# First seed requests on ScalarE's queue, and all seed stages three slots sooner, in a kernel of an S4D convolution beside softmax attention

## The chip, the cores and the metric

The kernel runs on one core of a Trainium2 chip. The metric is device time of one execution in microseconds, the lower the better. PE is TensorE, PEld its weight loads, DVE is VectorE, ACT is ScalarE, POOL is GpSimd and SP is SyncE, which here only requests DMA transfers. ACT can request transfers too, on a queue of its own.

## The reference

Two independent layers on sequences of 2048 with 448 channels, all in float32, concatenated at the end:

```python
dt = jnp.exp(log_dt)                                   # 448 step sizes
A = -jnp.exp(log_A_real) + 1j * A_imag                 # 448 x 256 poles
C = (C_real + 1j * C_imag) * dt[:, None]
P = jnp.exp((A * dt[:, None])[:, :, None] * pos[None, None, :])
K = 2.0 * jnp.einsum("dn,dnl->dl", C, P).real          # 448 x 2048 convolution kernel
y = irfft(rfft(u_t, L2) * rfft(K, L2), L2)[:, :, :L]   # causal convolution of u
a = y + u * D_skip
...
qkv = (x @ wqkv) ...                                   # 16 heads of 28
p = softmax(einsum("bhqd,bhkd->bhqk", q, k) * scale)
b = einsum("bhqk,bhkd->bhqd", p, v) ... @ wo
return jnp.concatenate([a, b], axis=-1)
```

## The kernel before

The kernel has three stages. In the opening stage it projects x to queries, keys and values and at the same time computes the seeds of the convolution kernel. In a short second stage (the maximum pass) it finds the row maxima of the first block of scores. In the main loop, 1054 of 1283 us, it does the attention and, in slots between the attention's steps, builds K from the seeds, transforms u and multiplies the spectra.

**The projections.** x comes in four parts of 512 rows (`load_x`, c = 0 to 3). Each part is transposed on PE (`transposes`), split into a high and a low half (`xh` by ACT, `xl` by DVE), and multiplied with the weights, which are split the same way: `khat` holds the halves of the query and key weights for now, in the space that later holds the first keys, and `vh`, `vl` those of the value weights. The weights arrive in two staging tiles of the pool name `tri`, which the seeds use later. A part gives 12 jobs, 48 in all: `qk_proj` for keys (s = 1) and queries (s = 0) of four groups, and four `v_proj`. What a job left in PSUM (`pm`) is evacuated behind the next job's matmuls: high half by ACT, low half by DVE (`hl`, in the last part `xn` for queries), then written to DRAM. For the keys of the first two parts a difference is made as well (`kb`, `dhl`), with POOL making the low half of it. Once the last matmul has read a group's weights, keys are loaded back into `khat`, four rows' requests for each of four indexes.

**The seeds.** The 448 channels are eight octets of 56. `seeds(o)` lists the stages of octet o: load four parameter arrays (`nat`), exponential and scaling by the step sizes (`exp_a`, `times_dt`), transposes to PSUM (`turn`, tile `pn`), phases and sizes (`phases`, `sizes`, both into a `tri` tile), `reduce`, `sines`, then `g_base` (POOL; `gz`), `places`/`e_base` (POOL, in `qhat` tiles), `e3` and `g_first` (DVE; `px`, `sg`), `e5` (POOL; `x_e`), `g_copies` (ACT; `sg`), and two writes to DRAM (`put_g`, `put_e`). Every octet needs two table loads of ACT, one for the exponential and one for the sine. The step sizes are made once for all octets: `exact_exp` computes their exponential by some twenty small DVE instructions on 8 x 56 numbers, `turn_dt` transposes it, and five copies fill `dt_all`.

**What sets the order.** The opening stage is written in slots (lines 534 to 583). Slot t first issues projection jobs until 48 (t + 1)/37 of them are out (`PW` = 37), then the seed stages that fall into it: stage i of octet o stands in slot 4 o + i (`SP` = 4), its load two slots ahead of the octet's first. So there are 41 slots; the last four hold only seed stages of the last octet. After slot 36 the last keys, values and the next query block are loaded. In this stage the order written is a priority: a planner with a cost model of its own sorts the instructions of each engine, in the end each engine runs its list in order. Only ACT's table functions are tied in program order (`in_order`). In the main loop the order written is kept on every engine.

SP requests nearly all transfers, in order: the identity, the first part of x, the weights, a column of ones, the step sizes (`log_dt`, tile `sg`), octet 0's four parameter arrays, then `pw2` (powers of two, which `phases` needs) and constants.

Of the kernel before, what the change touches and what calls it, by code (L numbers as in the profile page):

```python
# [18 lines left out]
D = 448  # L19

H = 16
DH = 28
G = 4
HG = H // G
# [3 lines left out]
CK = 112  # L28
NCK = D // CK
# [20 lines left out]
JF = DF // 4  # L50
NB = D // 8
NBF = NB // 2
NO = 8
BO = NB // NO
PO = BO * 8
LV = 11
# [34 lines left out]
def body(ctx, tc, a, out):  # L91
    nc = Engines(tc)
    nc.kept = KEPT["p"]
    x, wqkv, wo, u_a = a["B_x"][0], a["B_wqkv"], a["B_wo"], a["A_u"][0]
# [23 lines left out]
    sel = const.tile([128, HG], F32, name="sel")  # L118
    kones = const.tile([128, 1], F32, name="kones")
# [106 lines left out]
    with ExitStack() as st:  # L226
        sst, xst, wst = ExitStack(), ExitStack(), ExitStack()
        t_p = pool(sst, "t_p")
# [16 lines left out]
        load_x(0)  # L245
        w_g = k0_t[:CK].rearrange("p g (i s k h e) -> p i s k g h e", i=2, s=2, k=NCK, h=HG)
        vh = y_p.tile([CK, NCK, D], F32R, name="vh")
        vl = y_p.tile([CK, NCK, D], F32R, name="vl")
        nc.gpsimd.memset(k0_t[:CK].rearrange("p g (n e) -> p (g n) e", e=32)[:, :, DH:].bitcast(F32), 0.0)
        vst = [x_p.tile([128, H, 32], F32, name=f"vst{i}") for i in range(2)]  # L250
        for t in vst:
            nc.gpsimd.memset(t[:, :, DH:DH + 1], 1.0)
            nc.gpsimd.memset(t[:, :, DH + 1:], 0.0)
        wns = []
        for i in range(2):
            wn = t_p.tile([128, 3, LV, BO * 16], F32, name="tri", bufs=2).rearrange("p t k h -> p (t k h)")
            wn = wn[:CK, :2 * 3 * D].rearrange("p (k s d) -> p k s d", k=2, s=3)
            wns += [wn[:, 0], wn[:, 1]]
        for k in range(NCK):
            nc.sync.dma_start(wns[k], wqkv[k * CK:(k + 1) * CK, :].rearrange("p (s d) -> p s d", s=3))  # L260
# [5 lines left out]
        def load_nat(o):  # L266
            nats[o] = s_p.tile([PO, 4, 256], F32, name="nat", bufs=2)
            for i, n in enumerate(("A_log_A_real", "A_A_imag", "A_C_real", "A_C_imag")):
                nc.sync.dma_start(nats[o][:, i, :], bass.AP(tensor=a[n].tensor, offset=a[n].offset + first(o) * 256,
                                                            ap=[[256, JF // 4], [JF * 256, 4], [1, 256]]))  # L270
# [4 lines left out]
        ldt = next(small)  # L275
        t = a["A_log_dt"]
        for f in range(2):
            nc.sync.dma_start(ldt[4 * f:4 * f + 4, :].rearrange("o (j i) -> o j i", j=4), bass.AP(
                tensor=t.tensor, offset=t.offset + f * DF, ap=[[JF // 4, 4], [JF, 4], [1, JF // 4]]))
        load_nat(0)  # L280
        pw2 = s_p.tile([128, LV], F32, name="pw2")
        nc.sync.dma_start(pw2, a["pw2"])
        half_pi = s_p.tile([128, 1], F32, name="half_pi")
        nc.gpsimd.memset(half_pi, TWO_PI / 4)
        nc.sync.dma_start(sel, a["sel"])
        nc.sync.dma_start(w1, a["w1"])
        for k in range(NCK):
            for s in (1, 0):
                src = wns[k][:, s, :].rearrange("p (g h e) -> p g h e", g=G, e=DH)
                hi, lo = (w_g[:, i, s, k, :, :, :DH] for i in range(2))  # L290
                nc.scalar.activation(hi, src, AF.Copy)
                nc.vector.tensor_tensor(lo, src, hi.bitcast(F32), ALU.subtract)
            nc.scalar.activation(vh[:, k, :], wns[k][:, 2, :], AF.Copy)
            nc.gpsimd.tensor_tensor(vl[:, k, :], wns[k][:, 2, :], vh[:, k, :].bitcast(F32), ALU.subtract)

        def exact_exp(y, x_, shape):

# [22 lines left out]
        def turn_dt():  # L320
            dt_ps = ps_t.tile([128, CQ], F32, name="pt")[:PO, :NO]
            nc.tensor.transpose(dt_ps, dt_o, ident[:NO, :NO])
            for i, f in enumerate((1.0, 0.15915494309189535, 2.0, -2.0, -1.0)):
                nc.vector.tensor_scalar(dt_all[:, i, :], dt_ps, f, None, op0=ALU.mult)

        NH = BO * 16
        mul = lambda e, o_, x_, y_: e.tensor_tensor(o_, x_, y_, ALU.mult)
# [215 lines left out]

        ahead = collections.defaultdict(list)
# [624 lines left out]
```

## Time and profile before

| | us |
|---|---|
| median of 3 runs | 1283.33 |
| lowest, highest | 1280.13, 1284.64 |
| the profiled execution | 1284.67 |
| its span | 1282.8 |

| engine | busy us | share of the span |
|---|---|---|
| PE | 1223.7 | 95% |
| ACT | 967.8 | 75% |
| DVE | 925.5 | 72% |
| POOL | 843.4 | 66% |

The profile is of one execution. Its span runs from the first to the last instruction recorded; the execution's own time is 1.9 us longer. The views that are quoted are of four kinds. A row of the order of time has the start and the length in us, the engine, the operation, the tiles written and read (buffer numbers left out), the shapes, how many instructions were merged, and in brackets how long the engine idled ahead of it and what ended that. All rows name line 75, a helper through which every instruction goes, so tiles tell them apart. A row of a tile has a group's least, median and greatest length in ns, and the start of its first and last instruction. A row of stretches has the busy time of each engine in a part of the span. A row of the DMA requests has their count and the KB of each. SPq and ACTq stand for requests of transfers, whose length is that of the request and not of the transfer.

### The profile page before, as it was taken

What the parts mean: (1) busy time and instruction counts of PE and PEld (TensorE: products, weight loads), DVE (VectorE), ACT (ScalarE), POOL (GpSimd) and SP (SyncE); (2) the same over time, 40 slices, a digit from 0 to 9 for tenths busy, and PEclk for the clock granted to TensorE, in tenths of its full rate; (3) what the DMA queues carried; (4) which work ended last, traced back from release to release, by engine and by line L of the source; (5) the groups of instructions that cost most, each with busy time, mean ns of one, the idle gap of its engine ahead of it and who ended that gap; (6) DMA issues with size and microseconds to landing.
All of it is one profiled execution on the core that took longest, in us unless ns stands there. A gap on an engine that the chain in (4) does not pass through costs nothing.

```text
span 1282.8 us, 33335 instructions
## 1 busy us (share of the span) xinstructions
PE 1223.7 (95%) x12641; PEld 700.9 (55%) x12641; DVE 925.5 (72%) x2106; ACT 967.8 (75%) x2162; POOL 843.4 (66%) x728
## 2 busy tenths in 40 slices
PE   7988867999999999999999999999999999999987
PEld 5867754455555555555555555555555555544433
DVE  5788877787877787878778888888887645645111
ACT  4978856688888888888888888888887666656452
POOL 2466651798778888877689999989995222324321
PEclk9988888899999999999999999999999999999999
DMA  6767887446664544465533223432324533657665
GB/s 210 263 242 241 265 301 290 127 93 182 172 154 106 156 133 146 128 214 195 169 102 91 61 76 106 149 88 71 83 59 154 175 135 132 205 171 227 194 171 165
DMA packets 200089, 205.36 MB, mean 160 GB/s; under 512 B 95992, under 2 KB 158520, under 8 KB 197880
## 3 DMA queue, kind: packets, MB, share of 16 engines
q1 hardware_dynamic: 199720, 202.87, 51.4%
q8 instruction: 100, 1.64, 0.5%
q10 hardware_dynamic: 208, 0.36, 0.1%
q14 instruction: 61, 0.50, 0.1%
HBM read 120.73 MB, written 82.18 MB: 158 GB/s over the span
## 4 chain that ended last, share of the span: by engine, by line
PE 77%; DVE 7%; ACT 5%; POOL 5%; issue 3%; DMA 2%; SPq 0%; ACTq 0%; POOLq 0%; DVEq 0%
PE pm L75 44%; PE pss L75 16%; PE po L75 16%; POOL e L75 1%; ACT tri L75 1%; DVE mx L75 1%; ACT rl L75 1%; PE pt L75 1%; POOL qhat L75 1%; DVE sg L75 1%; DVE hl L75 1%; DVE tri L75 1%; POOL x_e L75 1%; DVE px L75 1%; POOL p L75 1%
## 5 line engine op out<-in xcount | busy, mean ns | idle before, releaser
L75 ACT ACTIVATE p<-pss 128x512 f32<-128x512 f32 x1024 | 561.4, 611 | 112.8 <-PE pss L75 108.5
L75 PE MATMUL pss<-qhat,khat 128*128 128x512 f32 x1024 | 402.7, 399 | 1.5 <-ACT p L75 1.4
L75 DVE TENSOR_REDUCE mx<-pm 128x1 f32<-128x512 f32 x480 | 308.6, 684 | 109.6 <-PE pm L75 107.5
L75 PE MATMUL pm<-khat,qhat 128*128 128x512 f32 x749 | 326.4, 439 | 5.3 <-ACT rl L75 3.0
L75 POOL TENSOR_TENSOR e<-e,sdb 128x256 f32<-128x256 f32 x168 | 201.9, 1202 | 108.1 <-ACT e L75 62.4
L75 PE MATMUL po<-p,v 128*32 128x512 f32 x2048 | 269.1, 594 | 0.0
L75 POOL TENSOR_TENSOR e<-e,eu 128x256 f32<-128x256 f32 x168 | 248.0, 1476 | 13.2
L75 PEld LDWEIGHTS pm<-khat,qhat 128*128 128x128 f32 x749 | 141.4, 189 | 201.3 <-ACT p L75 52.0
L75 DVE CUSTOM_DVE_ANT_0 rl<-pm,rl 128x512 f32<-128x512 f32 x259 | 178.4, 689 | 71.6 <-ACT rl L75 68.4
L75 PEld LDWEIGHTS pss<-qhat,khat 128*128 128x128 f32 x1024 | 190.4, 188 | 46.1 <-issue 10.8
L75 POOL TENSOR_TENSOR eu<-e,sdb 128x256 f32<-128x256 f32 x168 | 202.0, 1202 | 0.0
L75 POOL TENSOR_TENSOR p<-pr,pr 64x448 f32<-64x448 f32 x64 | 73.1, 1142 | 160.4 <-PE pm L75 135.2
L75 ACT ACTIVATE rl<-pm 128x512 f32<-128x512 f32 x259 | 157.1, 607 | 12.7 <-PE pm L75 7.9
L75 DVE TENSOR_TENSOR g<-g,zg 128x128 f32<-128x128 f32 x392 | 162.2, 414 | 3.4
L75 PE MATMUL pm<-kdif,qhat 128*128 128x512 f32 x249 | 101.1, 406 | 8.5 <-DVE xn L75 6.6
L75 PE MATMUL pm<-xh,khat 112*128 112x512 f32 x256 | 87.0, 422 | 9.2 <-DVE kb L75 4.4
L75 DVE TENSOR_TENSOR zg<-g,zg 128x128 f32<-128x128 f32 x224 | 87.9, 393 | 5.1
L75 PEld LDWEIGHTS pm<-e,g 128*32 128x32 f32 x3584 | 57.2, 109 | 43.8 <-issue 16.1
L75 DVE TENSOR_TENSOR pr<-pm,ub 128x448 f32<-128x448 f32 x64 | 37.0, 620 | 56.2 <-PE pm L75 41.8
L75 PE MATMUL pm<-e,g 128*32 128x64 f32 x3584 | 73.0, 222 | 1.9 <-POOL e L75 1.9
L75 ACT ACTIVATE y<-pm 128x448 f32<-128x448 f32 x48 | 26.5, 553 | 58.2 <-PE pm L75 34.1
L75 ACT ACTIVATE ub<-pm 128x224 f32<-128x224 f32 (+1 forms) x96 | 38.8, 450 | 39.9 <-PE pm L75 37.6
(134 smaller groups left out, 1465.5 us busy)
## 6 DMA issues: line engine op xcount, KB each, us to landing
sdb<-sd SPq DMA_DIRECT2D x55, 336.0 KB
qhat<-q SPq DMA_DIRECT2D x64, 256.0 KB
khat<-k SPq DMA_DIRECT2D x64, 256.0 KB
sd<-sg SPq DMA_DIRECT2D x8, 1456.0 KB
k<-hl SPq DMA_DIRECT2D x16, 512.0 KB
mw<-in_mw SPq DMA_DIRECT2D x16, 512.0 KB
sd<-qhat SPq DMA_DIRECT2D x8, 896.0 KB
yu_d<-ub SPq DMA_DIRECT2D x64, 112.0 KB
```

Source lines behind the costliest of these rows:

```text
L75: i = f(*args, **kw)
```

## The change

Five things change.

The requests for the step sizes and for octet 0's four arrays go out on ACT's queue, ahead of the first part of x and the weights on SP's. The memset of `half_pi` moves with them. The exponential of the step sizes is written ahead of the weights and their splits. `pw2` is requested before the column of ones. All seed stages stand three slots sooner (`SH` = 3): stage i of octet o in slot 4 o + i - 3, its load in slot 4 o - 5, nothing sooner than slot 0, so that octet 0's first four stages share slot 0, behind `turn_dt`. There are 38 slots instead of 41, and the projection jobs keep their slots.

```diff
-S0, SP, SW, SD, PW, E3 = 0, 4, 0, 5, 37, 8
+SP, SH, PW, E3 = 4, 3, 37, 8
...
+        def load_nat(o, queue=nc.sync):
+            nats[o] = s_p.tile([PO, 4, 256], F32, name="nat", bufs=2)
+            for i, n in enumerate(("A_log_A_real", "A_A_imag", "A_C_real", "A_C_imag")):
+                queue.dma_start(nats[o][:, i, :], bass.AP(...))
...
+        for f in range(2):
+            nc.scalar.dma_start(ldt[4 * f:4 * f + 4, :].rearrange("o (j i) -> o j i", j=4), bass.AP(
+                tensor=t.tensor, offset=t.offset + f * DF, ap=[[JF // 4, 4], [JF, 4], [1, JF // 4]]))
+        load_nat(0, nc.scalar)
+        half_pi = s_p.tile([128, 1], F32, name="half_pi")
+        nc.gpsimd.memset(half_pi, TWO_PI / 4)
...
+        dt8 = next(small)
+        exact_exp(dt8, ldt, [NO, PO])
+        dt_o = next(small)
+        nc.vector.tensor_copy(dt_o.rearrange("o (i j) -> o j i", j=4), dt8.rearrange("o (j i) -> o j i", j=4))
...
         load_x(0)
...
         for k in range(NCK):
             nc.sync.dma_start(wns[k], wqkv[k * CK:(k + 1) * CK, :].rearrange("p (s d) -> p s d", s=3))
-        nc.sync.dma_start(kones, a["kones"])
...
         pw2 = s_p.tile([128, LV], F32, name="pw2")
         nc.sync.dma_start(pw2, a["pw2"])
+        nc.sync.dma_start(kones, a["kones"])
...
-        n_stage = SP * (NO - 1) + len(stages[0])
+        n_stage = SP * (NO - 1) + len(stages[0]) - SH
...
-                slots[max(SP * o + (i or -2), 0)] += st_
-        slots[1].insert(0, turn_dt)
+                slots[max(SP * o + (i - SH if i else -2 - SH), 0)] += st_
+        slots[0].insert(1, turn_dt)
```

The lines that were taken from their old places (the same requests on SP's queue, and the text of `exact_exp` and `turn_dt`, which is unchanged) are left out.

More of the change, by code (lines that the diff above doesn't have):

```diff
@@ L324, in turn_dt @@
                 nc.vector.tensor_scalar(dt_all[:, i, :], dt_ps, f, None, op0=ALU.mult)
+        load_x(0)
+        w_g = k0_t[:CK].rearrange("p g (i s k h e) -> p i s k g h e", i=2, s=2, k=NCK, h=HG)
+        vh = y_p.tile([CK, NCK, D], F32R, name="vh")
+        vl = y_p.tile([CK, NCK, D], F32R, name="vl")
+        nc.gpsimd.memset(k0_t[:CK].rearrange("p g (n e) -> p (g n) e", e=32)[:, :, DH:].bitcast(F32), 0.0)
+        vst = [x_p.tile([128, H, 32], F32, name=f"vst{i}") for i in range(2)]
+        for t in vst:
+            nc.gpsimd.memset(t[:, :, DH:DH + 1], 1.0)
+            nc.gpsimd.memset(t[:, :, DH + 1:], 0.0)
+        wns = []
+        for i in range(2):
+            wn = t_p.tile([128, 3, LV, BO * 16], F32, name="tri", bufs=2).rearrange("p t k h -> p (t k h)")
+            wn = wn[:CK, :2 * 3 * D].rearrange("p (k s d) -> p k s d", k=2, s=3)
+            wns += [wn[:, 0], wn[:, 1]]
+        for k in range(NCK):
+            nc.sync.dma_start(wns[k], wqkv[k * CK:(k + 1) * CK, :].rearrange("p (s d) -> p s d", s=3))
+        pw2 = s_p.tile([128, LV], F32, name="pw2")
+        nc.sync.dma_start(pw2, a["pw2"])
+        nc.sync.dma_start(kones, a["kones"])
+        nc.sync.dma_start(sel, a["sel"])
+        nc.sync.dma_start(w1, a["w1"])
+        for k in range(NCK):
+            for s in (1, 0):
+                src = wns[k][:, s, :].rearrange("p (g h e) -> p g h e", g=G, e=DH)
+                hi, lo = (w_g[:, i, s, k, :, :, :DH] for i in range(2))
+                nc.scalar.activation(hi, src, AF.Copy)
+                nc.vector.tensor_tensor(lo, src, hi.bitcast(F32), ALU.subtract)
+            nc.scalar.activation(vh[:, k, :], wns[k][:, 2, :], AF.Copy)
+            nc.gpsimd.tensor_tensor(vl[:, k, :], wns[k][:, 2, :], vh[:, k, :].bitcast(F32), ALU.subtract)
         NH = BO * 16
```

35 lines of the change are left out of this document (2 added, 33 removed).

## The prediction

> **What bounds the kernel now.** I read the page's head first, then the busy time by stretch, because the change touches only the opening stage.
>
> ```profile
> span 1282.8 us, 33335 instructions
> 0.00:181.00 181.00, 158.00 (x705) 126.97 (x705) 138.31 (x266) 140.47 (x337) 93.44 (x131) 0.94 0.74 248
> 181.00:196.00 15.00, 2.54 (x5) 1.34 (x5) 11.71 (x25) 4.08 (x15) 13.77 (x20) 0.57 1.02 359
> 196.00:228.00 32.00, 26.20 (x79) 15.09 (x79) 22.21 (x67) 19.99 (x37) 0.82 (x1) 0.87 0.68 248
> 228.00:1282.00 1054.00, 1036.94 (x11852) 557.45 (x11852) 753.28 (x1749) 803.24 (x1776) 735.39 (x578) 1.00 0.47 140
> ```
>
> The columns are the stretch, its length, the busy time of PE, PEld, DVE, ACT and POOL, the granted clock, the DMA share and GB/s. From 228 us on PE is busy 1036.94 of 1054 us. That is the main loop; the change leaves its instructions and their order alone, so it only starts sooner or later. Up to 181 us PE does the projections and is busy 158.00 of 181 us. Between them lies a hole: in 181 to 196 us PE works 2.54 of 15 us, while DVE works 11.71 and POOL 13.77. What they do there is read in the order of time, first ACT's own, then PE's, then the DMA requests.
>
> ```profile
> 183.36 0.57 ACT L75 ACTIVATE sg<-pn 128x112 f32<-128x112 f32 x2 [3.54 <-DVE px L75]
> 186.88 0.39 ACT L75 ACTIVATE gz<-gz 128x224 f32<-128x224 f32 x1 [1.92 <-POOL gz L75]
> 187.18 0.54 ACT L75 ACTIVATE sg<-px 128x112 f32<-128x112 f32 x2
> 187.52 0.63 ACT L75 ACTIVATE xn<-pm 128x512 fp32r<-128x512 f32 x1
> 192.93 0.58 ACT L75 ACTIVATE sg<-pn 128x112 f32<-128x112 f32 x2 [4.78 <-DVE px L75]
> 195.01 0.57 ACT L75 ACTIVATE sg<-px 128x112 f32<-128x112 f32 x2 [1.50 <-DVE sg L75]
> 195.37 0.63 ACT L75 ACTIVATE rl<-pt 128x512 f32<-128x512 f32 x1
> ...
> 179.81 0.40 PE L75 MATMUL pm<-xl,khat 112*128 112x512 f32 x1
> 181.90 0.47 PE L75 MATMUL pt<-kdif,qhat 128*128 128x512 f32 x1 [1.70 <-issue]
> 188.93 0.79 PE L75 MATMUL pm<-kdif,qhat 128*128 128x512 f32 x1 [6.56 <-DVE xn L75]
> 196.06 1.53 PE L75 MATMUL pt<-khat,qhat 128*128 128x512 f32 x2 [5.05 <-ACT rl L75]
> ...
> 179.11 3.02 SPq L75 DMA_DIRECT2D khat<-k  x4
> 189.43 6.82 SPq L75 DMA_DIRECT2D khat<-k  x8
> ```
>
> The `sg` and `gz` copies are seed stages: those at 183.36 and 187.18 belong to octet 6, those at 192.93 and 195.01 to octet 7, the last. ACT runs in order, so two things stand behind them. The last projection's evacuation, `xn<-pm`, starts only at 187.52, and its DVE half holds PE for 6.56 us. The first `rl` of the maximum pass starts at 195.37, right behind octet 7's last copy, and holds PE for 5.05 us. So in this stretch the tail of the seeds ends last, not the matrix work. PE has no seed work in the hole at all.
>
> **The change part by part.** The sum is made against the profiled execution: 1284.67 us, 1.9 more than its span and 1.3 above the median of 1283.33. I carry differences over to the median.
>
> *How far three slots are.* The same step of the octets gives the pace.
>
> ```profile
> L75 DVE TENSOR_TENSOR tri<-pn,pw x8: 1425/1440/1444, 34.5 to 165.1; 128x1232 f32<-128x1232 f32 x8
> ```
>
> Eight octets lie 130.6 us apart from first to last, 18.7 us each, 4.66 us per slot; three slots are 14.0 us. The last copy at 195.58 would come at 181.6, as the projections end, instead of 15 us behind.
>
> *Step 1, the first requests.* Six requests (two for the step sizes, four of `nat`) leave SP's queue, where they stood behind the weights, and go out on ACT's queue ahead of x's and the weights' data.
>
> ```profile
> 1.19 0.93 SPq L75 DMA_DIRECT2D xn<-in_B_x  x2
> 4.66 2.23 PE L75 MATMUL pt<-ident,xn 128*112 128x128 f32 x8 [4.66 <-DMA xn<-in_B_x]
> 4.63 1.60 SPq L75 DMA_DIRECT2D sg<-in_A_log_dt  x2
> 6.28 1.02 SPq L75 DMA_DIRECT2D nat<-in_A_log_A_real  x1
> 9.52 0.83 SPq L75 DMA_DIRECT2D nat<-in_A_A_imag  x1
> 9.53 1.04 ACT L75 ACTIVATE khat<-tri 112x448 fp32r<-112x448 f32 x2 [2.44 <-DMA tri<-in_B_wqkv]
> ...
> nat<-in_A_log_A_real SPq DMA_DIRECT2D x8, 56.0 KB
> ...
> 4.60:9.10 4.50, 2.18 (x8) 1.38 (x8) 0.69 (x1) 0.60 (x1) 0.00 (x0) 1.00 0.98 296
> 9.10:13.80 4.70, 3.55 (x10) 2.89 (x11) 3.06 (x6) 3.98 (x8) 1.66 (x2) 1.00 1.02 264
> ```
>
> The DMA engines are full (0.98 and 1.02) while PE waits for the weights, so four times 56 KB ahead of them cost 224 KB at 264 GB/s, 0.85 us. Against this, SP gets those requests out of its way (its second `nat` request went out only as the first weights landed, 9.52 against 9.53), which releases `pw2`, the constants and the next x; none was waited for. The bounds are 0, if the seeds' rows run beside x without holding a weight, and +2.4, if a weight request must also wait for the step sizes to land: x itself landed at 4.66 after a request at 1.19, 3.5 us, so up to 1.5 us more. I take +0.9, nearest to the full DMA share.
>
> The Trainium skill's page "DMA: Bandwidth & Descriptors", section "Issuing engines are not separate DMA queues", says that requests of the scalar and the sync engine end on the same 16 DMA engines and interleave. By that rule the +0.9 is right; if ACT's queue were a way of its own it would be 0 and the total 0.9 us lower. The trace agrees as far as it goes: the share is already at 1.02 with one queue in use. On ACT the six requests take about 1.60 + 1.02 + 0.83 + 2 x 0.8 = 5.1 us by SP's own rows, about 6 us from the start. ACT's first copy that waits for weights is at 9.53, after 2.44 us of idling: hidden, with some 3 us to spare.
>
> *Step 2, the exponential ahead of the weights.*
>
> ```profile
> L75 DVE TENSOR_SCALAR sg<-sg x10: 167/175/180, 21.1 to 27.1; 8x56 f32<-8x56 f32 x10
> L75 DVE TENSOR_TENSOR sg<-sg x6: 196/204/643, 23.5 to 27.3; 8x56 f32<-8x56 f32 x6
> L75 DVE SCALAR_TENSOR_TENSOR sg<-sg x3: 203/204/204, 21.7 to 27.5; 8x56 f32<-8x56 f32 x3
> L75 DVE TENSOR_TENSOR khat<-tri,khat x8: 615/621/1575, 10.1 to 19.6; 112x448 fp32r<-112x448 f32 x8
> 28.33 0.45 DVE L75 TENSOR_SCALAR dt_all<-pt 56x8 f32<-56x8 f32 x5 [0.35 <-PE pt L75]
> ```
>
> 10 x 0.175 + 6 x 0.204 + 3 x 0.204 plus two copies of about 0.2 is 4.0 us of DVE, moved from 21 to 28 us to about 5 to 9 us, where DVE works 0.69 of 4.50. Behind it on DVE stand the first `xl` and the weights' low halves, made from 10.1 us on. If the step sizes landed as late as 6.5 us, the low halves would slip by 0.4 us; taken as 0. The freed 4 us at 21 to 28 us are filled again by the first octet's phases: 0. The step sizes' transpose and five copies now come before the first scaling, as they did; 0.
>
> *Step 3, all stages three slots sooner.* The tail leaves the hole. With nothing of the seeds ahead of them, the last evacuations follow the last projection at their own 0.6 and 0.7 us, and the maximum pass starts about 2 to 3 us after PE's last projection at 180.2 instead of at 196.06. Five of its 80 matmuls (16 tiles of five) were already done in the hole, worth 5/80 of 32 us, 2.0 us. So the gain is 196.06 - 2.0 - 183 = 11; less 1 us for matmuls that find their key rows still loading, 10 us. Ends: -14, the full three slots, and 0. The loads aren't late: the key rows of indexes 0 and 1 are requested from 179.11 on, each index feeds a quarter of the pass (8 us), and the eight requests at 189.43 serve indexes 2 and 3, needed 16 and 24 us in. The DMA share of 1.02 in the hole says that they can't come much sooner, which is why I do not take -14.
>
> The "TensorE: Matmul & The Clock Gate" page of the Trainium skill (section "Part 1: The HAM clock gate") says the array halves its clock after about 3.4 us of idling and needs as long to come back. The trace agrees: 0.57 in the hole. By the rule a gap of 2 to 3 us would keep the clock, and the pass would not begin with 3.4 us at half speed, an estimate by that page of up to 1.7 us more; the sum doesn't use it.
>
> *Step 4, what the moved work costs where it goes.* About 11.7 us of DVE, 13.8 of POOL and 4 of ACT move in under the projections, which leave 181 - 138.31 = 42.7, 87.6 and 40.5 us free. But engines run in order, and one wait of this kind is there already:
>
> ```profile
> 71.65 2.15 POOL L75 TENSOR_TENSOR x_e<-qhat 128x336 f32<-128x336 f32 x1 [1.32 <-DVE qhat L75]
> L75 POOL TENSOR_TENSOR dhl<-kb,dhl x8: 723/736/1003, 24.7 to 88.0; 128x256 fp32r<-128x256 f32 x8
> L75 POOL TENSOR_TENSOR gz<-tri x8: 653/936/1000, 41.7 to 186.2; 128x224 f32<-128x224 f32 x8
> 76.82 0.72 POOL L75 TENSOR_TENSOR dhl<-kb,dhl 128x256 fp32r<-128x256 f32 x1
> 77.57 0.38 ACT L75 ACTIVATE kb<-pm 128x256 f32<-128x256 f32 x1 [4.73 <-POOL dhl L75]
> 78.47 1.22 PE L75 MATMUL pm<-xh,khat 112*128 112x512 f32 x2 [4.39 <-DVE kb L75]
> ```
>
> A projection's `dhl` stood on POOL behind octet 1's powers, and PE lost 4.39 us. There are eight such `dhl`, from 24.7 to 88.0, all in the first two passes over x. Shifted seeds can meet more of them or miss this one: bounds -4.4 and +13 (three more). I take +2, half of one, since the first three or four lay ahead of the seeds' POOL work, which began at 41.7 and now begins some 14 us sooner.
>
> Sum: +0.9 + 0 - 10 + 2 = -7.1 us. Profiled 1284.67 - 7.1 = 1277.6; median 1283.33 - 7.1 = **1276.2 us**.
>
> **The rivals.**
>
> *The tail stays where the planner puts it.*
>
> ```profile
> 176.56 0.41 DVE L75 TENSOR_TENSOR qhat<-qhat 128x112 f32<-128x112 f32 x1
> ```
>
> This is octet 6's `e3` (program slot 33), 11.5 us behind octet 7's `tri<-pn,pw` at 165.1 (slot 32), and so octet 6's copies of slot 34 ran as late as 187.7. If the new last octet lags the same, its copies, now in slots 34 and 35, end one slot later than octet 6's did: 187.7 + 4.7 = 192.4 against 195.58, a gain of 3.2, less 0.9: -2.3 us, 1281.0. For it speaks that the lag arose under the projections, with three slots to go. Against it: POOL and DVE were half idle there, so the lag is one of order, and the planner sorts anew.
>
> *POOL's seeds get in the way of `dhl` (slower).* Place: 25 to 60 us. With POOL's seeds from about 28 us instead of 41.7, the `dhl` of the first pass meet the powers of octet 0, as one of the second pass met octet 1's. Price 4.39 us of PE each, as quoted. Beyond two more stalls than before the gain is gone; with four it is -9.1 + 17.6 = +8.5, 1291.8; with three, 1287.4. For it: the wait exists. Against: POOL is busy 93.44 of 181 us, and only one of eight was caught so far.
>
> *The seeds' requests aren't what starts the seeds.* The first `phases` writes a `tri` buffer that holds weights until their splits end, near 20.3 us (the last at 19.6). `tri<-pn,pw` can then move from 34.5 to about 21, 13.5 instead of 14.0 us: -6.6, 1276.7, inside the forecast.
>
> **How the numbers follow.** Forecast (5 to 11 us faster) 0.54; more, with the `dhl` stall missed, 0.06; tail still late (1 to 5 us faster) 0.19; POOL in the way (slower) 0.21. A measurement tells about 0.3%, 3.9 us, from no change. Faster: 0.54 + 0.06 + 0.04 of the late tail = 0.64. Within: the rest of the late tail and a little of the POOL case, 0.17. Slower: 0.19. The forecast's own range is 1272 to 1279; over all cases 1270.5 to 1287, leaving out most of the large POOL case and the very large gain.
>
> **What would show it.** Step 1: the first `khat<-tri` at 9.5 moves to about 10.4. Step 2: the `sg<-sg` group starts near 5 us, not 21. Step 3: `tri<-pn,pw` runs from about 20 to 151, the last `sg<-px` copy lies near 182, the first `rl` near 184, and PE in the 15 us behind the projections is busy over 10 us. Step 4: the waits of PE for `kb`, `hl` and `xl` sum to within 3 us of before. I would be wrong if PE's busy share up to the end of the projections fell, pushing that end beyond 186 us, or if ACT still copied `sg` ahead of the first `rl`.

## The result and the profile after

The change made the kernel faster by less than half of what was forecast, going by the measured ratio. It is 0.9975, 95% interval 0.9967 to 0.9983, which is 3.2 us; the forecast was 1276.2 us, a ratio of 0.9944, 7.1 us. The medians of nine runs each, 1283.33 us before and 1278.39 us after (1277.67 to 1279.79), lie 4.9 us apart; but in the later rounds the kernel before had medians of 1281.0 to 1281.7 us, which fits the smaller figure. The profiled executions differ by more, 6.2 us of span: the one of the kernel before, 1284.67 us, is the slowest of all its executions measured, so part of what the profiles show below as gained is the luck of that execution. The time after lies inside the range, and the gain is below the 0.3% that the prediction took as the least a measurement can tell.

The busy time by stretch, the kernel after, same columns as before:

```profile
span 1276.6 us, 33328 instructions
0.00:181.00 181.00, 154.88 (x681) 122.00 (x682) 141.04 (x277) 140.87 (x343) 104.51 (x144) 0.93 0.75 245
181.00:196.00 15.00, 11.98 (x43) 8.37 (x41) 9.55 (x23) 7.98 (x17) 6.05 (x6) 0.89 1.01 354
196.00:228.00 32.00, 25.02 (x78) 13.63 (x76) 23.41 (x70) 17.43 (x32) 0.43 (x1) 0.87 0.92 326
228.00:1276.00 1048.00, 1032.06 (x11844) 555.32 (x11843) 749.03 (x1740) 801.28 (x1771) 735.19 (x578) 1.00 0.48 139
```

The hole is filled: PE is busy 11.98 of the 15 us from 181 on, where it was busy 2.54. But up to 181 us it is busy 154.88 us, 3.1 less than before. Part of what fills the hole is projection work that came late. The order of time shows it, ACT's rows first and then PE's:

```profile
185.15 0.58 ACT L75 ACTIVATE sg<-pn 128x112 f32<-128x112 f32 x2 [0.29 <-DVE px L75]
187.76 0.57 ACT L75 ACTIVATE sg<-px 128x112 f32<-128x112 f32 x2 [2.03 <-DVE sg L75]
188.13 0.63 ACT L75 ACTIVATE xn<-pm 128x512 fp32r<-128x512 f32 x1
188.66 0.59 ACT L75 ACTIVATE rl<-pt 128x512 f32<-128x512 f32 x1
...
186.53 0.40 PE L75 MATMUL pm<-xl,khat 112*128 112x512 f32 x1
189.54 0.80 PE L75 MATMUL pm<-kdif,qhat 128*128 128x512 f32 x1 [2.37 <-DVE xn L75]
```

The last projection ends at 186.9 us instead of 180.2, the last copy of the seeds at 188.3 instead of 195.6, and the first `rl` starts at 188.66 instead of 195.37. ACT still has octet 7's copies ahead of the first `rl`; now projections and seeds end almost together. The start, in order of time and by tile:

```profile
10.27 1.04 ACT L75 ACTIVATE khat<-tri 112x448 fp32r<-112x448 f32 x2 [1.30 <-DMA tri<-in_B_wqkv]
17.78 0.90 ACT L75 ACTIVATE nat<-nat,dt_all 56x256 f32<-56x256 f32 x2
20.12 0.90 ACT L75 ACTIVATE nat<-nat,dt_all 56x256 f32<-56x256 f32 x2
...
L75 DVE TENSOR_SCALAR sg<-sg x10: 172/178/438, 2.8 to 6.4; 8x56 f32<-8x56 f32 x10
L75 DVE TENSOR_TENSOR tri<-pn,pw x8: 1422/1437/1456, 25.7 to 157.9; 128x1232 f32<-128x1232 f32 x8
```

The exponential runs at 2.8 us instead of 21. The eight octets' phases start 8.8 us sooner at the first and 7.2 us sooner at the last, not 14.

**One account for all kernels.** In every kernel below, the maximum pass ends 29 to 32 us behind the first `rl`, and 1056 to 1061 us follow. So most of what differs is when the first `rl` can start (it ranges over 34 us, the two stretches behind it over 3 and 5; with four slots it comes 7.4 us sooner than before, and the span is only 3.5 shorter). It starts behind the end of the projections and behind the last copy of the seeds, whichever is later. In the table, one profiled execution each: the end of the projections is the start of the last `pm<-xl,khat` matmul plus 0.4, the last copy that of the last `sg<-px` plus 0.4. "Waits" are PE's waits from 12 us to the projections' end. "Half clock" is an estimate of what PE lost by it: stretches of 2 us from 20 us on, 2 x (1 - granted clock) each, summed. Where PE waits within such a stretch, the time is counted in both columns.

| kernel | ratio to before, 95% | phases, first to last | projections' end | last copy | first `rl` | waits | half clock | span |
|---|---|---|---|---|---|---|---|---|
| before | 1 | 34.5–165.1 | 180.2 | 195.6 | 195.4 | 13.8 | 10.2 | 1282.8 |
| after (3 slots, early requests) | 0.9975 (0.9967–0.9983) | 25.7–157.9 | 186.9 | 188.3 | 188.7 | 18.0 | 11.9 | 1276.6 |
| early requests only | 0.9967 (0.9954–0.9980) | 26.2–163.5 | 177.5 | 187.9 | 187.7 | 12.3 | 8.5 | 1273.3 |
| 3 slots only | 1.0011 (1.0003–1.0020) | 32.7–164.3 | 192.9 | 193.5 | 193.8 | 25.2 | 11.9 | 1281.2 |
| after, `e3` on POOL | 0.9948 (0.9937–0.9960) | 26.3–157.0 | 184.7 | 177.8 | 185.3 | 18.5 | 10.2 | 1275.6 |
| after, requests on SP's queue | 0.9997 (0.9989–1.0006) | 31.0–162.6 | 190.1 | 191.5 | 191.8 | 23.0 | 6.8 | 1281.2 |
| 1 slot | 0.9936 (0.9923–0.9949) | 26.4–157.1 | 176.8 | 181.5 | 181.8 | 14.6 | 5.1 | 1269.1 |
| early only, `e3` on POOL | 0.9940 (0.9928–0.9952) | 26.5–162.3 | 176.8 | 185.8 | 185.6 | 15.0 | 5.1 | 1271.8 |
| one octet | one run, 1248.95 us | 26.3 | 160.9 | 50.2 | 161.4 | 5.7 | 5.1 | 1247.2 |
| exponential written late | 0.9981 (0.9972–0.9990) | 24.6–157.3 | 184.8 | 186.2 | 186.5 | 17.1 | 13.6 | 1275.8 |
| 2 slots | 0.9906 (0.9890–0.9922) | 24.9–153.2 | 175.2 | 177.0 | 177.4 | 15.2 | 5.1 | 1264.4 |
| 4 slots | 1.0001 (0.9992–1.0011) | 24.9–152.5 | 187.5 | 186.2 | 188.0 | 20.6 | 12.0 | 1279.3 |
| 1 slot, requests late | 0.9943 (0.9932–0.9954) | 33.0–159.4 | 179.0 | 183.7 | 184.0 | 14.9 | 5.1 | 1274.2 |
| 1 slot, `e3` on POOL | 1.0007 (0.9998–1.0015) | 26.6–169.8 | 190.2 | 193.4 | 193.7 | 22.6 | 15.4 | 1282.2 |
| octets 0–3: 2 slots, 4–7: 3 | 0.9943 (0.9923–0.9963) | 26.8–156.2 | 186.3 | 184.0 | 186.9 | 18.6 | 13.7 | 1276.4 |
| octets 0–3: 3 slots, 4–7: 2 | 0.9926 (0.9913–0.9939) | 26.7–152.1 | 179.2 | 182.3 | 182.6 | 15.6 | 5.1 | 1270.2 |
| octet 0: 2 slots, others 3 | 0.9943 (0.9928–0.9958) | 26.0–154.9 | 183.3 | 183.9 | 184.3 | 18.5 | 10.2 | 1271.1 |
| 2 slots, requests late | 0.9940 (0.9927–0.9952) | 31.7–155.6 | 179.0 | 181.8 | 182.1 | 16.6 | 8.6 | 1269.2 |

The projections' end less the two losses is 152 to 160 us in every kernel with all octets, while the end itself runs from 175 to 193. So more than half of what differs in that end is PE's waits and PE's time at half clock.

### The profile page after: what moved, and what is told of

It is laid out like the page before. It is cut to its first block, busy times and chain, and to the rows that moved or that the text cites. A ratio compares the mean times of both kernels' runs of the same rounds, so it can differ in the third digit from the quotient of the medians.

```text
span 1276.6 us, 33328 instructions
## 1 busy us (share of the span) xinstructions
PE 1223.9 (96%) x12641; PEld 699.3 (55%) x12641; DVE 923.0 (72%) x2106; ACT 967.5 (76%) x2162; POOL 846.2 (66%) x728
## 4 chain that ended last, share of the span: by engine, by line
PE 75%; DVE 8%; POOL 6%; ACT 4%; issue 3%; DMA 3%; SPq 0%; ACTq 0%; POOLq 0%; DVEq 0%
PE pm L75 43%; PE pss L75 16%; PE po L75 16%; POOL e L75 2%; DVE tri L75 1%; ACT rl L75 1%; POOL qhat L75 1%; DVE mx L75 1%; DVE sg L75 1%; POOL eu L75 1%; ACT tri L75 1%; DVE px L75 1%; DVE qhat L75 1%; DVE hl L75 1%; DMA sd<-qhat 1%
## 5 line engine op out<-in xcount | busy, mean ns | idle before, releaser
L75 POOL TENSOR_TENSOR e<-e,eu 128x256 f32<-128x256 f32 x168 | 248.2, 1477 | 13.2
L75 PEld LDWEIGHTS pm<-e,g 128*32 128x32 f32 x3584 | 57.2, 109 | 43.4 <-issue 17.1
L75 ACT ACTIVATE y<-pm 128x448 f32<-128x448 f32 x48 | 26.5, 553 | 58.2 <-PE pm L75 36.2
```

Source lines behind the costliest of these rows:

```text
L75: i = f(*args, **kw)
```

## The experiments

The parts first, then the number of slots, then what parts two slots from three. Edits are given against the changed kernel.

**The early requests alone** (the stages at their old slots).

```diff
-SP, SH, PW, E3 = 4, 3, 37, 8
+SP, SH, PW, E3 = 4, 0, 37, 8
-        slots[0].insert(1, turn_dt)
+        slots[1].insert(0, turn_dt)
```

> The requests on ACT's queue and the early exponential as in the change, the seed stages in their old slots (SH = 0, 41 slots, the step sizes' transpose in slot 1). Theory (the tail behind the projections is what pays, and only the shift moves it): the last copy into sg stays near 195, the first rl near 195, PE's last projection near 180 to 182; 1283 within 2 us, that is 0 to 1 us slower by the 0.9 us of later weights. Rival (an early start of octet 0 alone pulls all octets forward, since the planner starts what is ready): tri<-pn,pw begins near 26 and the last copy lies several us sooner, 1278 to 1280.

0.9967, as much as the whole change: the theory fell, and the rival's path held with a greater gain than it named. By tile:

```profile
L75 ACT ACTIVATE sg<-px x16: 354/392/434, 48.6 to 187.5; 128x112 f32<-128x112 f32 x16
L75 PE MATMUL pm<-xl,khat x128: 388/394/775, 12.6 to 177.1; 112*128 112x512 f32 x128
```

The last copy comes at 187.9 without any shift (188.3 in the changed kernel), and the projections end at 177.5, sooner than before. The gain of the change is that of its early requests; three slots on top added nothing that can be told from zero.

**The three slots alone** (the kernel before, but for `SH` and the slots; of the edit only the requests' lines are shown).

```diff
-            nc.scalar.dma_start(ldt[4 * f:4 * f + 4, :]...
+            nc.sync.dma_start(ldt[4 * f:4 * f + 4, :]...       # behind the weights, as before
-        load_nat(0, nc.scalar)
+        load_nat(0)
```

> The kernel before with the stages three slots sooner and nothing else; requests and exponential in their old places. Theory (the shift does it, the early requests only let the first octet start): octet 0 is held by its parameters (landing 9 to 16 us) and by the exponential behind the weights' splits, so tri<-pn,pw begins near 29 to 31 instead of 25.7, but the last octet is as early as in the change; 1278 to 1281. Rival (without the early requests the pipeline of octets starts late and stays late): tri<-pn,pw ends near 162 to 165, the first rl near 193 to 195, 1282 to 1285.

1.0011: no gain, as the rival had it. By tile, and PE's waits for `kb` up to the end of the projections (us, times, longest):

```profile
L75 DVE TENSOR_TENSOR tri<-pn,pw x8: 1421/1436/1442, 32.7 to 164.3; 128x1232 f32<-128x1232 f32 x8
L75 ACT ACTIVATE sg<-px x16: 349/400/458, 56.2 to 193.1; 128x112 f32<-128x112 f32 x16
L75 PE MATMUL pm<-xl,khat x128: 388/394/652, 13.1 to 192.5; 112*128 112x512 f32 x128
...
PE pm L75 <- DVE kb L75: 11.6, 4, 6.6
```

Three slots less in the text moved the phases by 1.8 us at the first octet and 0.8 at the last, and put the projections' end 12.7 us later. A slot is a priority and not a time. PE's waits for `kb` grew from 4.4 to 11.6 us. The longest, 6.60 us up to 50.92, had `kb` among seed instructions on ACT and DVE; in that of 4.07 us up to 101.29, ACT's `kb` waited 3.02 us for a `dhl` that stood on POOL behind an octet's powers. This is the wait that the prediction priced in its rival on POOL, and in this kernel it came.

**`e3` on POOL** in the changed kernel, to take work off DVE in the tail.

```diff
-SP, SH, PW, E3 = 4, 3, 37, 8
+SP, SH, PW, E3 = 4, 3, 37, 0
```

> The change with the six e3 instructions of every octet on POOL instead of DVE (E3 = 0). It takes some 20 us off DVE (48 instructions of 0.4 us and more) and the handovers from DVE to POOL ahead of e5. Theory (the 6.7 us by which the projections end later are waits of PE for DVE's evacuations, xl and hl, behind seed instructions): DVE's waits of PE fall from 14 to under 9 us, the projections end near 183 instead of 186.9, 1274 to 1277. Rival (the projections are late from the start, or from ACT, or the clock, and DVE's load has no part): the end stays at 186 to 188, 1278 to 1282, with POOL's chain 20 us longer as a further risk.

0.9948, within the time expected. ACT's rows in order of time, and one group of PE's waits up to the end of the projections (line and what it waited for: us, times, longest):

```profile
177.21 0.59 ACT L75 ACTIVATE sg<-px 128x112 f32<-128x112 f32 x2 [0.19 <-DVE sg L75]
184.78 0.60 ACT L75 ACTIVATE xn<-pm 128x512 fp32r<-128x512 f32 x1 [2.16 <-PE pm L75]
185.27 0.59 ACT L75 ACTIVATE rl<-pt 128x512 f32<-128x512 f32 x1
...
PE pm L75 <- ACT vst L75: 6.0, 4, 1.9
```

Here the tail is out of the way, 10.5 us sooner than in the changed kernel, and the first `rl` still starts only at 185.27, behind the last projection. Drawing in the tail by 10.5 us was worth little by itself: the first `rl` moved by 3.4 us, of which 2.2 are the earlier end of the projections. The theory's reason fell, though its time was met: PE's waits for DVE went from 13.2 to 10.1 us, not under 9, and its waits for ACT from 4.8 to 8.4 us (`vst`, the values' evacuation, from 1.1 to 6.0), so all waits together stayed at 18.

**The requests on SP's queue**, still ahead of x.

```diff
-            nc.scalar.dma_start(ldt[4 * f:4 * f + 4, :]...
+            nc.sync.dma_start(ldt[4 * f:4 * f + 4, :]...
-        load_nat(0, nc.scalar)
+        load_nat(0)
```

> The change with the six early requests on SP's queue, still ahead of x and the weights. Theory (the queue matters little, since the same transfer engines carry it): SP issues them for about 5 us ahead of x, so x lands near 8 to 9 instead of 4.7 and the first weights near 14; 3 to 4 us slower than the change if that delay is not absorbed, 1281 to 1283. Rival (the start is absorbed, because the seeds' tail and not the projections ends the stage): within 1 us of the change, 1278 to 1279.

0.9997 against 0.9975: 2.8 us worse, near what the theory had. SP's requests and PE's first work in order of time:

```profile
1.89 1.01 SPq L75 DMA_DIRECT2D nat<-in_A_log_A_real  x1
5.52 1.04 SPq L75 DMA_DIRECT2D xn<-in_B_x  x2
...
9.02 2.19 PE L75 MATMUL pt<-ident,xn 128*112 128x128 f32 x8 [9.02 <-DMA xn<-in_B_x]
```

x was requested 4.3 us later (1.19 before) and landed 4.3 us later than in the changed kernel, at 9.02 instead of 4.72. The Trainium skill, page "DMA: Bandwidth & Descriptors", section "Issuing engines are not separate DMA queues", says that starting transfers on several engines saves only the time that a sequencer needs to start them. This agrees: the six requests took SP from 1.19 to 5.5 us, and that is what the second queue saved.

**One octet only.** The seeds of octets 1 to 7 are left out (7/8 of the seeds' work); their writes to DRAM remain, with octet 0's data.

```diff
+        for o in range(1, NO):
+            stages[o] = [[] for _ in stages[0]]
+            stages[o][-2] = [...]        # put_g of octet 0's tile
+            stages[o][-1] = [...]        # put_e of octet 0's tile
```

> The change with seeds for octet 0 alone; the other seven octets write octet 0's seeds to DRAM in their places, so seven eighths of the seed work is left out and everything behind it is the same work. It prices the seeds as a whole. Theory (both the late end of the projections and the tail are the seeds'): the projections end near 170 (their matmuls are 158 us up to there, and the start costs 10), the first rl follows within 3 us, the whole is 15 to 20 us below the change, 1259 to 1264. Rival (the projections are held by their own evacuations and transfers): they end at 178 or later, 1268 or more.

By tile:

```profile
L75 PE MATMUL pm<-xl,khat x128: 389/399/795, 12.9 to 160.5; 112*128 112x512 f32 x128
L75 ACT ACTIVATE rl<-pt x13: 592/597/601, 161.4 to 187.8; 128x512 f32<-128x512 f32 x13
```

With little beside them the projections end at 160.9, well before the 170 that I had expected, and the first `rl` follows 0.9 us after the last projection began. The other seven octets cost the changed kernel 27 us ahead of its first `rl`. This is the room that any order of these stages works in, and PE's own share of the seeds is part of it.

**The exponential written behind the weights again**, its requests still early.

```diff
-        exact_exp(dt8, ldt, [NO, PO])        # ahead of load_x(0)
+        exact_exp(dt8, ldt, [NO, PO])        # behind the weights' splits
```

> The change with the exponential of the step sizes written where it was before, behind the weights' splits; the requests stay early on ACT's queue, the shift stays 3. Theory (octet 0's start counts, and the exponential is what held it: it ran from 21.1 to 28 us): sg<-sg again from about 20, tri<-pn,pw from 30 to 34, the last copy 3 to 6 us later than in the change, 1281 to 1284, no better than before. Rival (the parameters' arrival was what held it): tri<-pn,pw from 26 to 28, 1277 to 1279.

0.9981, the interval overlapping the changed kernel's; the time is the rival's. The exponential still ran from 2.8 to 6.4 us: at these two places in the text the planner starts it when its data are there.

**One, two and four slots**, all with the early requests; and one slot with late requests.

```diff
-SP, SH, PW, E3 = 4, 3, 37, 8
+SP, SH, PW, E3 = 4, 1, 37, 8        # or 2, or 4
```

> The change with the stages one slot sooner instead of three (SH = 1). New theory (the octets run at their own pace of some 19 us from the moment the first can start, whatever slots they stand in, and a greater shift only puts their instructions ahead of the projections'): tri<-pn,pw begins at 25 to 27 as with 0 and 3, the last copy into sg lies at 185 to 188, and the projections end between the 177.5 of shift 0 and the 186.9 of shift 3; 1275 to 1278, between shift 0 and the change. Rival (the planner's order is a lottery, and each shift draws another): no order in the shift; the end of the projections or the last copy outside 177 to 188, the time outside 1274 to 1279.

> The change with SH = 2. With SH = 0, 1 and 3 the projections ended at 177.5, 176.8 and 186.9 us and the last copy into sg at 187.9, 181.5 and 188.3. Theory (a shift first shortens the tail, then holds up the projections: their PE waits and the half-clock stretches behind them grow with it): projections end at 178 to 184, last copy 181 to 187, the PE time lost to the half clock ahead of that end between the 5.1 us of SH = 1 and the 11.8 of SH = 3; 1273 to 1277. Rival (each shift draws an order of its own): anything from 1271 to 1281, with end and lost clock outside those bounds.

> The change with SH = 4, the most that fits ahead of the last loads (37 slots). Theory (more shift, more hold-up): projections end at 187 to 192, no tail behind them (last copy at most 2 us later), 1279 to 1284. Rival (an order drawn anew): below 1277, or the projections ending before 184.

> The kernel before with the stages one slot sooner and nothing else (SH = 1, requests and exponential in their old places). It completes the pairs: SH = 0 late is the kernel before, SH = 0 early 4 us faster than it, SH = 3 late 1.4 us slower, SH = 3 early 3 us faster, SH = 1 early 8 us faster. Theory (the early start of octet 0 is what pays, by some 4 to 5 us at any shift, and one slot adds 3 to 4 on top): tri<-pn,pw from 33 to 34, last copy near 189 to 191, 1277 to 1279. Rival (the single slot alone does it): 1273 to 1275.

0, 1, 2, 3 and 4 slots with early requests give 0.9967, 0.9936, 0.9906, 0.9975 and 1.0001. Two slots are the best kernel of this study, 1269.63 us median, faster than both. Both expectations missed it (1273 to 1277 us, and 1271 or more by the rival). One slot came out below its theory's range, where the rival of an order drawn anew had put it; for four slots the theory held. By tile:

```profile
L75 DVE TENSOR_TENSOR tri<-pn,pw x8: 1418/1432/1444, 24.9 to 153.2; 128x1232 f32<-128x1232 f32 x8
L75 ACT ACTIVATE sg<-px x16: 347/394/423, 51.0 to 176.6; 128x112 f32<-128x112 f32 x16
L75 PE MATMUL pm<-xl,khat x128: 389/394/775, 12.3 to 174.8; 112*128 112x512 f32 x128
```

With early requests and up to two slots the last copy moves roughly as the prediction had it: 187.9, 181.5, 177.0, that is 6.4 and 10.9 us against 4.7 and 9.3 by the pace. With three it goes back to 188.3, and the projections' end goes from 175.2 to 186.9. With late requests the pace fits nowhere: with 0, 1, 2 and 3 slots the last copy lies at 195.6, 183.7, 181.8 and 193.5, so the first slot alone moves it by 11.9 us. With one slot, early and late requests differ by 0.7 thousandths, their intervals overlapping: one slot alone, without the early requests, gives 0.9943, more than the whole change, as its rival had it.

**`e3` on POOL with no shift and with one slot.**

```diff
-SP, SH, PW, E3 = 4, 3, 37, 8
+SP, SH, PW, E3 = 4, 0, 37, 0        # or 4, 1, 37, 0
```

> Requests and exponential early, stages in their old slots (SH = 0), and e3 on POOL (E3 = 0): the two that did best put together. Theory (a short tail of the last octet and projections that aren't held up add): projections end near 178, last copy near 180 to 184 instead of 187.5, 1272 to 1275, some 2 us faster than either. Rival (both take the same time away, since the maximum pass waits for the key rows and for DMA once it starts that early): 1275 to 1277, as either alone.

> SH = 1 early, with e3 on POOL (E3 = 0). On SH = 3 that took about 3 us off, on SH = 0 about 3. Theory (DVE's queue holds the last octet's tail and the evacuations): 1270 to 1272, last copy near 178 to 180. Rival (the tail already ends 5 us behind the projections at SH = 1, and what then starts the maximum pass are the key rows): 1272 to 1275, no faster than without.

The same edit gains 2.7 thousandths with three slots (0.9975 to 0.9948) and 2.7 with none (0.9967 to 0.9940), and loses 7.1 with one (0.9936 to 1.0007). So it is no fixed cost of DVE or POOL; I read it as the order that comes out, which is not shown further. With one slot both expectations missed by 8 us or more; with none the time was as expected, though the last copy moved only to 185.8 (expected near 180 to 184).

**What parts two slots from three.** Three mixtures, and two slots with late requests.

```diff
+        sh = lambda o: 2 if o < 4 else 3        # or 3 if o < 4 else 2, or 2 if o < 1 else 3
-                slots[max(SP * o + (i - SH if i else -2 - SH), 0)] += st_
+                slots[max(SP * o + (i - sh(o) if i else -2 - sh(o)), 0)] += st_
```

> Octets 0 to 3 two slots sooner, octets 4 to 7 three, the rest as in the change. Theory (what parts two slots from three arises in the first four octets, whose phases already differ by the fifth, 96.4 us against 104.6): projections' end 175 to 179 us, last copy of the step sizes 176 to 181, 1264 to 1268 us in the profile, ratio 0.990 to 0.993. Rival A (it arises in the last four): projections' end 184 to 188 us, ratio 0.996 to 0.999. Rival B (each order falls where it falls, and no part of it carries the difference): either end can lie outside both bands, with the half-clock time anywhere from 5 to 15 us.

> Octets 0 to 3 three slots sooner, octets 4 to 7 two. Theory (the first four octets carry it): projections' end 184 to 188 us, ratio 0.996 to 0.999. Rival A (the last four): 175 to 179 us, ratio 0.990 to 0.993. Rival B (each order falls where it falls): both this run and its mirror image on the same side, or outside the bands.

> Octet 0 alone two slots sooner, octets 1 to 7 three as in the change. Theory (three slots are worse than two because octet 0's stages then pile up in the first slot, where nothing earlier is left for them to move to): projections' end back to 175 to 179 us, ratio 0.990 to 0.993. Rival A (the pile-up is no part of it): 184 to 188 us, ratio 0.996 to 0.999. Rival B (each order falls where it falls): outside both bands.

> Two slots sooner with the requests and the exponential where they were before. Theory (the early requests are worth what they take off the start of octet 0's phases, 8 us less what PE loses to it, at every shift): 3 to 5 us longer than two slots with early requests, ratio 0.993 to 0.995, phases from about 33 us. Rival (the early requests bring something only where the tail is the last to end, as without a shift, and little where the projections end last or beside it): within 1.5 us of two slots with early requests, ratio 0.990 to 0.992.

From two slots (0.9906), three in the last four octets alone give 0.9943, three in the first four alone 0.9926, at the edge of the error. From three slots (0.9975), octet 0 alone put back to two gives 0.9943, the interval clear of the changed kernel's. By the projections' end in single profiles (186.3 and 179.2) the last four octets would seem to carry the difference; by the ratios they carry about half of it. So my theory, that the first four carry it, fell, and that the last four alone do isn't borne out: the parts cost some 4.7 us (the last four) and 2.6 us (the first four), and octet 0's third slot, which piles its stages up in the first, costs some 4 us where the others stand at three. None of the three ends and ratios fell into its theory's bands together. Two slots with late requests are 3.4 thousandths (4.4 us) worse than with early ones, as the theory had it.

**The same order, three profiles.** The first mixture ran between 1269.3 and 1278.2 us with one list of instructions on each engine, so it was profiled twice more, unchanged.

> The kernel with octets 0 to 3 two slots sooner and 4 to 7 three, unchanged: its executions lay between 1269.3 and 1278.2 us with one and the same order, and the profiled one was at the upper end (span 1276.4 us, projections' end 186.3 us, 13.7 us lost at half clock). Theory (what varies from execution to execution is how much PE loses at half clock): in a profile of span S the loss is 13.7 - (1276.4 - S) within 2 us, so 6 to 9 us at 1270. Rival (the waits vary, by when transfers land, and the clock follows or does not): the loss stays 11 us or more and PE's waits fall from 18.6 us by the difference.

> The same kernel for a third profile, same reading: the loss at half clock follows the span one for one within 2 us (theory), or stays while the waits of PE take the difference (rival). If the span comes out within 1.5 us of one already seen, it tells nothing more.

Spans of 1276.4, 1270.4 and 1272.9 us; lost at half clock 13.7, 10.2 and 10.3; PE's waits 18.6, 18.4 and 17.9. In the third profile the loss accounts for the difference (3.4 of 3.5 us); in the second for 3.5 of 6.0, outside the 2 us I allowed, with another 0.8 from the first projections, which came sooner there. The waits hardly vary. The stretches below show the same wait of PE in two profiles, for `xl`, 1.87 us up to 148.13 and 1.92 us up to 145.21 (columns as in the first fence), first in the slowest execution, then in the second:

```profile
146.00:148.00 2.00, 0.26 (x2) 0.00 (x0) 2.00 (x5) 1.97 (x4) 1.84 (x3) 1.00 0.63 156
148.00:150.00 2.00, 1.87 (x12) 1.77 (x13) 2.00 (x6) 1.46 (x3) 1.69 (x3) 0.90 0.26 74
150.00:152.00 2.00, 2.00 (x8) 1.34 (x8) 1.82 (x3) 2.00 (x5) 1.29 (x3) 0.50 0.00 0
...
156.00:158.00 2.00, 2.00 (x7) 1.78 (x6) 1.97 (x3) 0.55 (x1) 0.00 (x0) 0.50 0.65 227
158.00:160.00 2.00, 2.00 (x8) 1.77 (x6) 2.00 (x6) 1.51 (x5) 0.94 (x1) 0.54 0.38 119
```

```profile
144.00:146.00 2.00, 0.79 (x5) 0.80 (x5) 2.00 (x6) 1.90 (x2) 1.61 (x3) 0.82 0.62 177
146.00:148.00 2.00, 2.00 (x10) 1.75 (x8) 2.00 (x5) 0.60 (x1) 2.00 (x4) 0.50 0.06 21
148.00:150.00 2.00, 2.00 (x14) 1.57 (x12) 0.96 (x2) 1.71 (x5) 0.33 (x1) 0.83 0.00 0
```

In the one the clock stays at half for some 10 us, in the other for some 3.4.

## Why the prediction was right or wrong

**What bounds.** Right. The first `rl` was held by the tail of the seeds, and all that was gained was gained there: the first `rl` moved by 6.7 us, the span by 6.2.

**Step 1, the first requests.** The cost was of the size forecast: `khat<-tri` starts at 10.27 instead of 9.53, +0.7 for +0.9. But it is no finer than the executions vary: that start lies between 9.5 and 10.1 us in the profiles with late requests and between 9.6 and 10.5 in those with requests early on ACT's queue. Its gain was not in the sum at all. The requests alone move the phases of octet 0 from 34.5 to 26.2 and the last copy from 195.6 to 187.9, and gave 0.9967; the sum had put the tail's whole gain under step 3. How much they bring depends on the order around them: 4.4 us with two slots (0.9940 to 0.9906), 4.6 with three (1.0011 to 0.9975), within the error with one.

**Step 2, the exponential.** Right at 0. It ran at 2.8 us, 2 us sooner than I had said, with the same effect.

**Step 3, the three slots.** This term failed: it was -10 us, and the runs put the three slots at nothing or a small loss (0.9967 to 0.9975 with the requests early, 1 to 1.0011 without). One and two slots show that a shift can draw the tail in. But "three slots are 14.0 us" took the pace of the octets for the size of a slot. The first octet can't start before its data: with 0 to 4 slots and early requests its phases come at 24.9 to 26.4 us. In the changed kernel they were expected from about 20 us and came at 25.7: octet 0's scaling by the step sizes ran on ACT at 17.78 and 20.12, between the weights' splits. The last octet's phases move, but not in proportion: 163.5, 157.1, 153.2, 157.9 and 152.5 us with 0 to 4 slots. With three they were expected at 151 and came at 157.9, and from there to the last copy it took 30.4 us, as before (30.5); with two slots it took 23.8. So the tail moved 7.3 us, not 14, and the requests alone had moved it by 7.7. Why the octets lie 18.7 us apart is not shown: every kernel here has four slots per octet. The rival "the tail stays where the planner puts it" was nearer to this than the forecast, and "the seeds' requests aren't what starts the seeds" fell: with three slots and no early requests the phases begin at 32.7.

**Step 4, what the moved work costs.** This step failed too: with +0.9 and -10 as they stood, an end of the projections 6 us later alone would have brought the sum from -7.1 to about -3. It was sized +2 from one kind of stall; the projections' end moved by 6.7 us, of which step 1 explains 0.7. The end passed the 186 us that the prediction named as its undoing. The groups of PE's waits up to the end of the projections (line and what it waited for: us, times, longest), the kernel after and then the kernel before:

```profile
PE pm L75 <- DVE hl L75: 6.8, 6, 2.6
PE pt L75 <- DVE xl L75: 5.0, 4, 2.7
PE pm L75 <- DVE kb L75: 1.4, 3, 0.9
```

```profile
PE pm L75 <- DVE kb L75: 4.4, 1, 4.4
PE pt L75 <- DVE xl L75: 3.2, 2, 2.6
PE pm L75 <- DVE hl L75: 2.0, 4, 0.9
```

The stall on `dhl` that I had priced and multiplied is gone, and its rival, "POOL's seeds get in the way of `dhl`", did not come about in this kernel (it did, in part, with the three slots alone). The loss came from kinds I had not priced: the projections' own evacuations standing behind seed work on DVE. The sum of the three groups went from 9.6 to 13.2, past the 3 us I had allowed. That DVE's load is the cause is not shown: with `e3` off DVE its waits fell by 3.1 us and ACT's took their place. The three longest waits of the kernel after, each PE row with what stood on the other engine ahead of it; the first, for `nat`, has a fellow of 2.7 us in the kernel before and is no part of the loss:

```profile
54.77 0.70 PE L75 MATMUL pn<-ident,nat 56*128 56x56 f32 x8 [2.76 <-ACT nat L75]
60.83 1.10 PE L75 MATMUL pt<-ident,xn 128*112 128x128 f32 x4 [2.65 <-DVE xl L75]
94.23 0.74 PE L75 MATMUL pm<-vh,xh 112*128 112x448 f32 x1 [2.57 <-DVE hl L75]
...
53.05 1.28 ACT L75 ACTIVATE tri<-tri,half_pi 128x1232 f32<-128x1232 f32 x1
54.23 0.49 ACT L75 ACTIVATE nat<-nat,dt_all 56x256 f32<-56x256 f32 x1
...
58.15 0.56 DVE L75 TENSOR_TENSOR sg<-pn,tri 128x224 f32<-128x224 f32 x1 [2.42 <-POOL tri L75]
...
60.11 1.27 DVE L75 TENSOR_TENSOR xl<-pt,xh 112x512 fp32r<-112x512 f32 x2
...
89.83 1.96 DVE L75 TENSOR_TENSOR tri<-tri 128x1232 f32<-128x1232 f32 x1
...
93.50 0.68 DVE L75 TENSOR_TENSOR hl<-pm,hl 128x512 fp32r<-128x512 f32 x1
```

`xl` of the second part of x stood on DVE behind a seed stage that itself waited 2.42 us for POOL; `hl` at 93.50 stood behind the sines' 1.96 us and what followed. And the clock goes down around such waits; the stretches of the kernel after:

```profile
92.00:94.00 2.00, 0.00 (x0) 0.00 (x0) 2.00 (x5) 0.60 (x2) 0.38 (x1) 0.92 0.35 120
94.00:96.00 2.00, 1.77 (x5) 1.60 (x6) 1.40 (x4) 1.99 (x2) 0.00 (x0) 0.50 0.43 127
...
100.00:102.00 2.00, 2.00 (x10) 1.70 (x8) 0.24 (x1) 1.40 (x6) 1.93 (x4) 0.88 0.53 162
```

With the wait of 2.57 us come some 6.8 us at half clock, 3.4 us of PE's work. Against the kernel before, waits grew by 4.2 us and the loss at half clock by 1.7, together 5.9 of the 6.7. Against two slots the end is 11.7 us later, and 2.8 of waits and 6.8 of half clock account for 9.6 of it.

**The two steps together.** They do not add: with the projections ending at 186.9, a tail that had moved the full 14 us, to 181.6, would have brought the first `rl` at most some 1.2 us more: it started 0.6 us behind the projections' end with `e3` on POOL, and 1.8 us behind it in the changed kernel.

**What stays open.** Why three slots give an order with more and longer waits than two is not settled beyond the mixtures: both halves and the first octet carry a part. I found no rule in the text of the kernel that predicts 0.9906 for two slots and 0.9975 for three, nor why one slot draws the tail in by 11.9 us with late requests and by 6.4 with early ones. Part of each difference between single profiles, a few us, is also the length of the half-clock stretches in that execution.

## What to carry to other kernels

Where a planner sorts the instructions, a place in the text is a priority: read from the trace how far a step can move (its data, the engine's list) before turning slots into microseconds, and ask of the early data and the early place separately which of them brings the gain. Two chains that end together must both be priced, since the later of them sets the time and drawing in one only uncovers the other. And try the neighbours of a shift by one or two: here a smaller one gave almost four times the gain.

## What the runs showed of the hardware

Waits of PE of 2.57 to 2.76 us were followed by half clock (those at 54.77 and 60.83 us in the kernel after by a granted clock of 0.50 to 0.53 from 56 to 66 us), in stretches of about 3.4 us or a small multiple of that, so that the losses in the table come in steps of about 1.7 us (5.1, 6.8, 8.5, 10.2, 11.9, 13.6). The length of the single wait does not decide it: in the kernel after, 1.59 us up to 168.29 was followed by 0.50 from 170 to 172 us, 1.27 us up to 133.52 was not (1.00 to 138 us), and the 0.50 from 80 to 82 us has no wait of over 0.9 us in the 4 us ahead of it. The Trainium skill, page "TensorE: Matmul & The Clock Gate", section "Part 1: The HAM clock gate", says that the gate looks at free-running windows of about 3.4 us and halves the clock after an idle one. The length of the stretches and their varying from one execution to the next, about 3.4 and about 10 us behind the same wait (1.92 and 1.87 us), agree with it; that waits shorter than a window did it, and that the clock stayed at half through stretches with PE busy 2.00 of 2.00 us (150 to 158 us in the slowest profile above), goes beyond that rule. My prediction had used the rule only for the hole, where it changed nothing in the sum; it weighed more under the projections.
